# Lightning attention and a leaky-ReLU feed-forward on one core: heads in memory order, and eight more GpSimd dependencies

## The chip, the core and the metric

The kernel runs on one core of a Trainium2 chip. The time is device microseconds of one execution; the figure for a kernel is the median of several runs. A core has a matrix engine (TensorE, PE in the profile, with its weight loads as PEld), VectorE (DVE), ScalarE (ACT), GpSimd (POOL) and SyncE (SP), which here issues the DMA transfers.

## The reference

Linear attention with a decay per head, block by block, then a feed-forward layer on the heads side by side. All results are float32; w_in and w_out come as float64.

```
B, H, S, D = 4, 8, 768, 64            # q, k, v; block = 64
for each block b of a sequence:
    intra = (qb @ kb.T) * Dmask       # Dmask[i, j] = lam ** (i - j) for i >= j
    out   = intra @ vb + (qb * lam ** (i + 1)) @ kv_state
    kv_state = lam ** 64 * kv_state + (kb * lam ** (63 - j)).T @ vb
x = out, heads side by side           # (3072, 512)
h = x @ w_in                          # (512, 2048)
y = max(0.01 * h, h) @ w_out          # (2048, 512)
```

## The kernel before

The 3072 tokens are 24 chunks of 128 (two blocks each, six chunks a sequence, four sequences). Four chunks make a group of 512 tokens.

**Attention of a chunk.** `load_kq` and `load_v` bring k, q and v of a chunk (128 tokens by 8 heads by 64). k and q come in two transfers each: the even heads into the first four places of the tile, the odd heads behind them; v comes in one, in memory order. `transposes` turns k and q on TensorE, two heads side by side on the 128 partitions (in later chunks other transfers and VectorE do it for q, and later for k). `scores` has two TensorE steps: `go` (q times k) and `kv` (k times v, the addition to the state). `outputs` has three: `own` (scores times v), and `inter(0)` and `inter(1)` (state times scaled q), between which an engine reads a corner of the result (`seen_po`). In a steady chunk TensorE runs `own`, `inter(0)`, then `kv` and `go` of the next chunk, then `inter(1)`.

All these steps are made of calls of `quad` (L410), a plain f32 matmul of 64 rows by 64 columns. `rows` (0 or 1) picks the upper or lower 64 partitions of both inputs, `cols` those of the output. A call so uses one of four quarters of the array. The sequence in which the calls are written is the sequence in which TensorE gets them.

`place(h)` says where head h lies in the transposed tiles: which half of the partitions (`a`), which of the four columns (`z`). `own` sends head 2y + hi to the output half hi; `inter(m)` takes those calls for which `t = y % 2 ^ m`.

Around it, GpSimd (VectorE in some early chunks) scales k for the state (`kr`, L591), GpSimd multiplies the state by the decay (L653) and, in later chunks, scales q (L598). VectorE masks the scores (L643), adds to the state (L650) and splits the output into parts for the feed-forward (`xh` on ScalarE, `xl`, `xm`). At the start `factors` (L380) copies `lam` into `lam_h` in the order of the heads, `factors_k` (L383, L386) and `factors_q` (L391, L393) make the tables of decay powers by scans.

**Feed-forward.** Every operand is split into three parts of reduced precision (h, l, m), so each product is three matmuls of 512 columns (`up`, L856; `down`, L922). `to_float32` brings a piece of w_in or w_out as float64 (L787, L790) and turns it into float32 on ScalarE (L799 to L803) and VectorE (L805, L806); `parts` makes the three parts (L813 to L820). The weights' keys in the plan are `w320`, `w321` for the raw pieces and `wh0`, `wl0`, `wm0` and so on for the parts. The result of `up` goes to DRAM and comes back for `down`.

**Order.** All operations are registered by `add(engine, us, fn, reads, writes, ...)` with a planner, `Plan`. `ORDER` lists operations by number and engine, 1296 entries; `emit` takes these first, in this order, and places the rest by planned times. `resolve` turns `reads` and `writes` into dependencies, which the planner uses for its times and for naming buffers. At the end it issues the instructions:

```
for _, _, i, e in self.timeline:
    ...
    fn() if len(ways) == 1 else fn(e)
```

Waits between engines come from the tiles that an instruction itself reads and writes; each engine runs its instructions in the order in which they were issued.

Of the kernel before, what the change touches and what calls it, by code (L numbers as in the profile page):

```python
# [239 lines left out]
def kernel(  # L240
# [27 lines left out]
    FIRST_LOADS = ["k0", "q0", "v0", "k1", "q1", "v1", "w10", "k2", "q2", "v2", "w11", "k3", "q3", "v3"]  # L268
    LOW_PE, MIX_PE = set(), set()
    PAIRS = {"q": set()}  # L270
    QS = 8
    KM = 8
    NRAW = 3
    TURN = 3
    SLACK, GSLACK = 4.0, 2.0
    EARLY_SLACK = 1.0
    GOFIRST = 3
    SUBL, FIRST = 0.75, -8.0

    DV, QD = 10, 8  # L280
    RUNS = {8: (-8.0, 0.8), 10: (-8.0, 0.8), 12: (4.0, 0.0)}
    C4 = P // 4
    HALF = (slice(0, D), slice(D, 2 * D))
    assert NCB % TURN == 0 and D == 64 and KO == HP == 4 and SEQ % C == 0 and NCH % GC == 0 and d_model == T == 512 and NP % 4 == 0

    pool = ctx.enter_context(tc.tile_pool(name="sb", bufs=1))
    psum = ctx.enter_context(tc.tile_pool(name="ps", bufs=1, space=bass.MemoryType.PSUM))
    dram = ctx.enter_context(tc.tile_pool(name="dram", bufs=1, space=bass.MemoryType.DRAM))
    ctx.enter_context(tc.manual_schedule(engines=None))

    def sb(shape, name, dt=F32):
        return pool.tile(shape, dt, name=name, tag=name)
# [27 lines left out]
    def part(n):  # L320
        nonlocal used
        used += n
        assert used <= NA, used
        return att[:, used - n:used]

    ident = part(P)
    kqv_f = [part(2 * H * D + (TURN - 2) * HP * C * (i == 1)) for i in range(3)]
    kqv = [[x[:, i * H * D:(i + 1) * H * D].rearrange("p (h d) -> p h d", h=H) for i in range(2)] for x in kqv_f]
    kTs, qTs, qsTs = ([part(HP * C).rearrange("p (y t) -> p y t", y=HP) for _ in range(2)] for _ in range(3))
    sc = part(2 * HP * C2).rearrange("p (x y t) -> p x y t", x=2, y=HP)  # L330
    state = [part(HP * D).rearrange("p (y d) -> p y d", y=HP) for _ in range(4)]
    decay = part(2 * HP * C2).rearrange("p (x y t) -> p x y t", x=2, y=HP)
    pow_q = part(HP * C2).rearrange("p (y t) -> p y t", y=HP)
    lam_b, lam_h = part(H), part(H)
    lam_p = part(HP)
    zero = part(1)
    seen_po = part(2)
    eye = sc[:, 0, 0, :]


    nc.scalar.dma_start(out=lam_b, in_=lam.partition_broadcast(P))
    make_identity(nc, ident)

    def busy(n, at):

        wide = bank[at].rearrange("p (a t) -> p a t", t=C2)
# [20 lines left out]
    def move(us, fn, reads, writes, issue=0.5, rank=0.0, slack=SLACK, name=None, land=None):  # L367

        if name in FIRST_LOADS:
            rank = FIRST_LOADS.index(name) * 0.01 - 100.0 - plan.rank  # L370
        plan.slack = slack if steady else EARLY_SLACK
        if steady and not rank:
            rank = FIRST
        add("DMA", length(us, issue), fn, reads, writes, rank=rank, land=land or us)
        plan.slack = 0.0


    def factors():
        for i in range(2):
            nc.vector.tensor_copy(lam_h[:, i * HP:(i + 1) * HP], lam_b[:, i::2])  # L380

    def factors_k():
        nc.vector.tensor_tensor(eye, ident[:, 0:C2], ident[:, C2:C], op=ALU.add)  # L383
        for hi in range(2):
            for hp in range(HP):
                nc.vector.tensor_tensor_scan(decay[:, hi, hp, :], _bc(lam_h[:, 2 * hp + hi], 1, C2), eye, 0.0,  # L386
                                             op0=ALU.mult, op1=ALU.add)

    def factors_q():
        for i in range(2):  # L390
            nc.vector.tensor_copy(lam_p[HALF[i]], lam_h[HALF[i], i::2])  # L391
        for hp in range(HP):
            nc.vector.tensor_tensor_scan(pow_q[:, hp, :], _bc(lam_p[:, hp], 1, C2), _bc(zero[:, 0], 1, C2), 1.0,  # L393
                                         op0=ALU.mult, op1=ALU.add)

    pow_k = decay[:, :, :, C2 - 1].rearrange("p hi hp -> p hp hi")
    lam_c = pow_q[:, :, C2 - 1]
    plan.rank = -1.0
    add("DVE", 0.25, factors, [], ["lam"])
    add("DVE", 1.65, factors_k, ["lam"], ["fk", "sc"])  # L400
    add("DVE", 1.2, factors_q, ["lam"], ["fq"])
    if LOW_PE or MIX_PE:
        add("ACT", 0.2, lambda: nc.scalar.activation(out=neg_i, in_=ident, func=AF.Copy, bias=0.0, scale=-1.0), [], [f"wm{LATE_W}", "neg_i"])
    if MIX_PE:
        add("ACT", 0.2, lambda: nc.scalar.activation(out=pos_s, in_=ident, func=AF.Copy, bias=0.0, scale=S), [], [f"wm{LATE_W}", "pos_s"])
    ENG = {"ACT": nc.scalar, "DVE": nc.vector, "POOL": nc.gpsimd}


    def quad(dst, rows, lhsT, rhs, cols, start=False):
        nc.tensor.matmul(dst[HALF[cols]], lhsT=lhsT[HALF[rows]], rhs=rhs[HALF[rows]], start=start, stop=True,  # L410
                         skip_group_check=True)
# [4 lines left out]
    def place(h):  # L416
        i = h // 2 + h % 2 * HP
        return i % 2, i // 2
# [26 lines left out]
    def load_pair(nm, c):  # L445
        b, n, i = of(c)
        y, (dst, keys) = (q if nm == "q" else k)[b, :, n * C:(n + 2) * C, :], pair(nm, c)

        def go():
            for z in range(2):  # L450
                nc.sync.dma_start(out=dst[:, z * HP:(z + 1) * HP].rearrange("p h s d -> p h (s d)"),
                                  in_=y[z::2].rearrange("h (p s) d -> p h (s d)", s=2))
        move(1.75, go, [], keys, issue=1.0, name=f"{nm}{c}")

    def load_kq(c):
        b, n, i = of(c)
        for src, x, nm in ((k, 0, "k"), (q, 1, "q")):
            if paired(nm, c):
                if c % 2 == 0:
                    load_pair(nm, c)  # L460
                continue
            y, (dst, key) = src[b, :, n * C:(n + 1) * C, :], spot(nm, c)

            def go(y=y, dst=dst):
                for z in range(2):
                    nc.sync.dma_start(out=dst[:, z * HP:(z + 1) * HP, :], in_=y[z::2].rearrange("h p d -> p h d"))
            if nm == "k" or c < QD:
                move(1.15, go, [], [key], issue=1.0, name=f"{nm}{c}")
# [33 lines left out]
    def load_subs(c):  # L502
        b, n, i = of(c)
        count = run(c)[1]
        for nm, src, pieces in zip("kq", (k, q), subs(c, count)):
            for sub, lo, hi, keys in pieces:
                add("DVE", 0.0, lambda: None, [], keys)
                for y in range(lo, hi):
                    for a in range(4):
                        h = y // 2 + (2 * y + a // 2) % HP * 2  # L510
                        z = src[b, h, n * C:(n + count) * C, a % 2 * C4:(a % 2 + 1) * C4]
                        o = sub[a * C4:(a + 1) * C4, y - lo, :]
                        move(0.55, lambda o=o, z=z: nc.sync.dma_start(
                                out=o.rearrange("j (m i) -> j m i", i=C4), in_=z.rearrange("(m j) i -> j m i", j=C4)),
                            keys, [f"{nm}s{y}{a}"], issue=SUBL, rank=RUNS.get(c, (4.0, 0.4))[0] + RUNS.get(c, (4.0, 0.4))[1] * (4 * y + a))
# [19 lines left out]
    def transposes(c):  # L535
# [41 lines left out]
        def copies():  # L577
# [3 lines left out]
            if c < DV:  # L581
                ways = (("ACT", "DVE"), (0.6, 0.685)) if c < GC else ("ACT", 0.6)
                add(*ways, lambda e="ACT": copy(e, into, src()), [key], [f"kT{i}"])
                if paired("q", c):
                    add(*ways, lambda e="ACT": copy(e, joined(qTs[i]), apart(zq())), [qkey], [f"qT{i}"])
                elif c < QD:
                    add(*ways, lambda e="ACT": copy(e, qTs[i], zq()), [qkey], [f"qT{i}"])
            kr = tk.rearrange("p (y x) d -> p y x d", x=2)
            nr = slice(0, C2 if n == NCB - 1 else P)
            add(*((("DVE", "POOL"), (0.67, 1.06)) if c < KM else ("POOL", 1.06)),  # L590
                lambda e="POOL": ENG[e].tensor_tensor(kr[nr], kr[nr], _bc(pow_k, 3, D)[nr], op=ALU.mult), ["fk"], [kk], lock=True)  # L591
            m = slice(1 if n == 0 else 0, 2)
            first = c < QS
            eng, e, us, dep = ("DVE", nc.vector, 0.685, [qkey, f"qT{i}"]) if first else ("POOL", nc.gpsimd, 1.28, [f"qT{i}"])

            def scale():
                o, x = (y.rearrange("p y (t i) -> p y t i", t=2)[:, :, m, :] for y in (qsTs[i], zq() if first else qTs[i]))
# [146 lines left out]
    def round_of(c):  # L744
# [18 lines left out]
        if c + 2 < NCH:  # L763
            load_v(c + 2)


    w_in_r = moe_w_in.rearrange("(ko ki) n -> ki ko n", ki=P)
    n_raw = 0

    def to_float32(kind, p, h, dst, key, after=()):  # L770
# [278 lines left out]
```

## Time and profile before

| | |
|---|---|
| median of 3 runs | 607.87 us (606.57, 607.87, 608.01) |
| profiled execution | 605.63 us |
| its span, first to last instruction | 603.8 us |
| TensorE busy | 596.2 us (99%) |
| VectorE, ScalarE, GpSimd busy | 299.1, 209.1, 73.9 us |
| granted TensorE clock | 0.999 |
| DMA engines, mean share in the first 34 us | 0.95 |

A row of a list of groups gives line, engine, operation, written and read tiles, shape, count, then busy time, mean time of one in ns, idle time before and what ended it. The tile `att` holds all of attention's buffers; `po`, `psc`, `pt` and `b` are accumulators. In the chain of waits a row is start, length, engine, tile, line and count; in the timeline it is start, length, then the instruction. A plain f32 matmul shows as two instructions.

### The profile page before, as it was taken

What the parts mean: (1) busy time and instruction counts of PE and PEld (TensorE: products, weight loads), DVE (VectorE), ACT (ScalarE), POOL (GpSimd) and SP (SyncE); (2) the same over time, 40 slices, a digit from 0 to 9 for tenths busy, and PEclk for the clock granted to TensorE, in tenths of its full rate; (3) what the DMA queues carried; (4) which work ended last, traced back from release to release, by engine and by line L of the source; (5) the groups of instructions that cost most, each with busy time, mean ns of one, the idle gap of its engine ahead of it and who ended that gap; (6) DMA issues with size and microseconds to landing.
All of it is one profiled execution on the core that took longest, in us unless ns stands there. A gap on an engine that the chain in (4) does not pass through costs nothing.

```text
span 603.8 us, 12715 instructions
## 1 busy us (share of the span) xinstructions
PE 596.2 (99%) x5362; PEld 491.9 (81%) x5362; DVE 299.1 (50%) x410; ACT 209.1 (35%) x322; POOL 73.9 (12%) x85
## 2 busy tenths in 40 slices
PE   8899999999999999999999999999999999999997
PEld 5788888888888888887888888888888888888886
DVE  6899854450553524344267855353453543534430
ACT  3686752222434433435334421222312313214111
POOL 3332132241322031230000000000000000000000
PEclk9999999999999999999999999999999999999999
DMA  9998887598788798655975834434333333433201
GB/s 215 226 274 214 237 226 201 96 251 202 197 227 215 230 247 233 171 199 194 323 250 194 294 105 132 148 101 139 108 120 125 122 122 123 127 101 128 82 1 69
DMA packets 149993, 105.18 MB, mean 174 GB/s; under 512 B 125872, under 2 KB 126640, under 8 KB 149936
## 3 DMA queue, kind: packets, MB, share of 16 engines
q1 hardware_dynamic: 149648, 104.30, 59.4%
q8 instruction: 42, 0.69, 0.5%
q14 instruction: 15, 0.12, 0.1%
q10 hardware_dynamic: 288, 0.07, 0.0%
HBM read 68.69 MB, written 35.65 MB: 173 GB/s over the span
## 4 chain that ended last, share of the span: by engine, by line
PE 96%; DVE 2%; DMA 0%; issue 0%; ACT 0%; DVEq 0%
PE b L856 33%; PE b L922 16%; PE psc L922 11%; PE po L922 11%; PE pt L856 11%; PE pt L922 5%; PE po L410 4%; PE psc L410 3%; DMA att<-in_lam_dram 0%; PE po L550 0%; PE b L550 0%; DVE att L393 0%; DVE att L386 0%; DVE w L806 0%; DVE att L643 0%
## 5 line engine op out<-in xcount | busy, mean ns | idle before, releaser
L904 DVE SCALAR_TENSOR_TENSOR xl<-att,xh 128x1024 fp32r<-128x1024 f32 x48 | 58.7, 1222 | 125.8 <-ACT xh L903 125.8
L903 ACT ACTIVATE xh<-att 128x1024 fp32r<-128x1024 f32 x48 | 50.9, 1061 | 147.5 <-PE po L922 73.9
L856 PE MATMUL b<-xl,wl 128*128 128x512 f32 (+1 forms) x296 | 78.1, 389 | 0.1
L856 PE MATMUL b<-xm,wm 128*128 128x512 f32 (+1 forms) x296 | 77.9, 390 | 0.0
L856 PE MATMUL b<-xh,wh 128*128 128x512 f32 (+1 forms) x296 | 77.5, 389 | 0.0
L883 ACT ACTIVATE gs<-b 128x512 f32<-128x512 f32 x73 | 42.9, 597 | 95.3 <-PE b L856 85.7
L856 PEld LDWEIGHTS b<-xl,wl 128*128 128x128 f32 x296 | 54.7, 188 | 12.0 <-DVE wl L820 0.9
L856 PEld LDWEIGHTS b<-xh,wh 128*128 128x128 f32 x296 | 54.6, 188 | 11.5 <-DVE att L598 0.3
L856 PEld LDWEIGHTS b<-xm,wm 128*128 128x128 f32 x296 | 54.4, 188 | 11.3
L906 DVE SCALAR_TENSOR_TENSOR xm<-xl,xh 128x1024 fp32r<-128x1024 f32 x48 | 58.8, 1226 | 4.7
L922 PE MATMUL b<-wh,xh 128*128 128x512 f32 x144 | 56.0, 389 | 0.0
L922 PE MATMUL b<-wl,xl 128*128 128x512 f32 x144 | 56.0, 389 | 0.0
L922 PE MATMUL b<-wm,xm 128*128 128x512 f32 x144 | 56.0, 389 | 0.0
L653 POOL TENSOR_TENSOR att<-att 128x256 f32<-128x256 f32 x40 | 29.8, 745 | 112.5 <-DVE att L650 74.0
L922 PE MATMUL psc<-wm,xm 128*128 128x512 f32 (+1 forms) x100 | 38.2, 387 | 0.0
L922 PE MATMUL po<-wm,xm 128*128 128x512 f32 (+1 forms) x100 | 37.9, 384 | 0.0
L922 PE MATMUL psc<-wh,xh 128*128 128x512 f32 x96 | 37.3, 389 | 0.0
L922 PE MATMUL psc<-wl,xl 128*128 128x512 f32 x96 | 37.3, 389 | 0.0
L922 PE MATMUL po<-wh,xh 128*128 128x512 f32 x96 | 37.3, 389 | 0.0
L922 PE MATMUL po<-wl,xl 128*128 128x512 f32 x96 | 37.3, 389 | 0.0
L410 PEld LDWEIGHTS po<-att 64*64 64x64 f32 x1408 | 26.9, 134 | 10.5 <-issue 7.8
L410 PE MATMUL po<-att 64*64 64x64 f32 x1408 | 32.9, 222 | 1.8 <-issue 1.1
(103 smaller groups left out, 859.1 us busy)
## 6 DMA issues: line engine op xcount, KB each, us to landing
att<-g SPq DMA_DIRECT2D x48, 512.0 KB, 3.4
g<-gs SPq DMA_DIRECT2D x47, 512.0 KB, 3.5
raw<-in_moe_w_in_dram SPq DMA_DIRECT2D x16, 512.0 KB, 5.5
raw<-in_moe_w_out_dram SPq DMA_DIRECT2D x16, 512.0 KB, 4.5
out_dram<-gs SPq DMA_DIRECT2D x23, 256.0 KB, 2.1
att<-in_k_dram SPq DMA_DIRECT2D x44, 128.0 KB, 4.0
att<-in_v_dram SPq DMA_DIRECT2D x22, 256.0 KB, 4.2
wo<-w SPq DMA_DIRECT2D x8, 512.0 KB, 3.9
```

Source lines behind the costliest of these rows:

```text
L410: nc.tensor.matmul(dst[HALF[cols]], lhsT=lhsT[HALF[rows]], rhs=rhs[HALF[rows]], start=start, stop=True, skip_group_check=True)
L653: add("POOL", 0.62, lambda new=new, j=j: nc.gpsimd.tensor_tensor(state[(j + 1) % 4], new, _bc(lam_c, 2, D), op=ALU.mult), [f"st{j % 4}", " ...
L856: nc.tensor.matmul(dst, lhsT=w[z][:, kk * 2 * P + f * P:kk * 2 * P + (f + 1) * P], rhs=x[z][:, kk, toks], start=start and kk == 0, stop=kk ...
L883: add("ACT", ns, lambda b=b, r=r: nc.scalar.activation(out=r(), in_=b(), func=AF.Prelu, bias=0.0, scale=1.0, alpha=0.01), [kb], [kg], rank ...
L903: add("ACT", 1.05, lambda: nc.scalar.activation(out=h, in_=graw[j], func=AF.Copy, bias=0.0, scale=NEAR), reads, wr("h"))
L904: add("DVE", 1.215, lambda: nc.vector.scalar_tensor_tensor(l, graw[j], 1.0, h.bitcast(F32), op0=ALU.mult, op1=ALU.subtract), reads + [f"rh ...
L906: add("DVE", 1.215, lambda: nc.vector.scalar_tensor_tensor(m, l.bitcast(F32), -S, h.bitcast(F32), op0=ALU.mult, op1=ALU.add), [f"rh{j}", f ...
L922: nc.tensor.matmul(to[:, cols], lhsT=ring[j][z][:, f * T + tb * P:f * T + (tb + 1) * P], rhs=W[pp][z][:, f * d_model:(f + 1) * d_model][:, ...
```

## The change

k and q of a chunk stay in memory order and come in one transfer each, so `place` and `lam_h` go, and head 2y + a lies in half a, column y of the transposed tiles. `own` sends head h to the output half `column(h)`, and `inter` takes the calls with `t = a ^ m`. The output's heads so lie in other halves for odd y, and the rows of w_in follow: each piece of it is loaded in two transfers of 64 partitions. `BEHIND` names, for three k scalings and five state products on GpSimd, a part of the weights that is added to their `reads`. In `ORDER` five GpSimd entries stand elsewhere among the other engines' (87, 126, 134, 205, 207); taken engine by engine, the order of both lists is the same.

```diff
-    ORDER = [...]
+    ORDER = [...]
...
+    BEHIND = {("k", 2): ["w320"], ("s", 7): ["wm0"], ("k", 5): ["wl0"], ("s", 9): ["wl2"], ("k", 6): ["wl2"], ("s", 12): ["wl3"], ("s", 13): ["wh4"], ("k", 8): ["wl4"]}
...
-    lam_b, lam_h = part(H), part(H)
+    lam_b = part(H)
...
-    def factors():
-        for i in range(2):
-            nc.vector.tensor_copy(lam_h[:, i * HP:(i + 1) * HP], lam_b[:, i::2])
-
...
-                nc.vector.tensor_tensor_scan(decay[:, hi, hp, :], _bc(lam_h[:, 2 * hp + hi], 1, C2), eye, 0.0,
+                nc.vector.tensor_tensor_scan(decay[:, hi, hp, :], _bc(lam_b[:, 2 * hp + hi], 1, C2), eye, 0.0,
...
-            nc.vector.tensor_copy(lam_p[HALF[i]], lam_h[HALF[i], i::2])
+            nc.vector.tensor_copy(lam_p[HALF[i]], lam_b[HALF[i], i::2])
...
-    add("DVE", 0.25, factors, [], ["lam"])
+    add("DVE", 0.0, lambda: None, [], ["lam"])
...
-    def place(h):
-        i = h // 2 + h % 2 * HP
-        return i % 2, i // 2
+    def column(h):
+        return h % 2 ^ h // 2 % 2
...
-                for z in range(2):
-                    nc.sync.dma_start(out=dst[:, z * HP:(z + 1) * HP, :], in_=y[z::2].rearrange("h p d -> p h d"))
+                nc.sync.dma_start(out=dst, in_=y.rearrange("h p d -> p h d"))
...
-                        h = y // 2 + (2 * y + a // 2) % HP * 2
+                        h = 2 * y + a // 2
...
-                lambda e="POOL": ENG[e].tensor_tensor(kr[nr], kr[nr], _bc(pow_k, 3, D)[nr], op=ALU.mult), ["fk"], [kk], lock=True)
+                lambda e="POOL": ENG[e].tensor_tensor(kr[nr], kr[nr], _bc(pow_k, 3, D)[nr], op=ALU.mult), ["fk"] + BEHIND.get(("k", c), []), [kk], lock=True)
...
-                        h = y // 2 + (2 * y + x) % HP * 2
-                        quad(pu[t]()[:, y, :], t, tk[:, 2 * y + x, :], tv[:, h, :], x, start=y == 0)
+                        h = 2 * y + x
+                        quad(pu[t]()[:, y, :], t, tk[:, h, :], tv[:, h, :], x, start=y == 0)
...
-                        [f"st{j % 4}", "fq"], [f"st{(j + 1) % 4}"], lock=True)
+                        [f"st{j % 4}", "fq"] + BEHIND.get(("s", j), []), [f"st{(j + 1) % 4}"], lock=True)
...
         def own():
             for y in range(HP):
-                for hi in range(2):
+                for a in range(2):
                     for t in range(2):
-                        h = 2 * y + hi
-                        a, z = place(h)
-                        quad(po[:, t, y, :], t, tv[:, h, :], sc[:, a, z, :], hi, start=y == 0)
+                        h = 2 * y + a
+                        quad(po[:, t, y, :], t, tv[:, h, :], sc[:, a, y, :], column(h), start=y == 0)
 
         def inter(m):
             for y in range(HP):
-                t = y % 2 ^ m
-                for hi in range(2):
+                for a in range(2):
+                    t = a ^ m
                     if n or t:
-                        a, z = place(2 * y + hi)
-                        quad(po[:, t, y, :], a, state[(2 * c + t - 1) % 4][:, z, :], qsT[:, z, tokens(t)], hi)
+                        quad(po[:, t, y, :], a, state[(2 * c + t - 1) % 4][:, y, :], qsT[:, y, tokens(t)], column(2 * y + a))
...
-    w_in_r = moe_w_in.rearrange("(ko ki) n -> ki ko n", ki=P)
+    w_in_r = moe_w_in.rearrange("(ko ki) n -> ki ko n", ki=C2)
...
-                nc.sync.dma_start(out=r64.rearrange("p (k f) -> p k f", k=2),
-                                  in_=w_in_r[:, 2 * h:2 * h + 2, p * 2 * P:(p + 1) * 2 * P])
+                o = r64.rearrange("p (k f) -> p k f", k=2)
+                for u, rows in enumerate((slice(4 * h, 4 * h + 4, 3), slice(4 * h + 1, 4 * h + 3))):
+                    nc.sync.dma_start(out=o[HALF[u]], in_=w_in_r[:, rows, p * 2 * P:(p + 1) * 2 * P])
```

More of the change, by code (lines that the diff above doesn't have):

```diff
@@ L449, in go @@
         def go():
-            for z in range(2):
-                nc.sync.dma_start(out=dst[:, z * HP:(z + 1) * HP].rearrange("p h s d -> p h (s d)"),
-                                  in_=y[z::2].rearrange("h (p s) d -> p h (s d)", s=2))
+            nc.sync.dma_start(out=dst.rearrange("p h s d -> p h (s d)"), in_=y.rearrange("h (p s) d -> p h (s d)", s=2))
         move(1.75, go, [], keys, issue=1.0, name=f"{nm}{c}")
@@ L464, in go @@
             def go(y=y, dst=dst):
-                for z in range(2):
-                    nc.sync.dma_start(out=dst[:, z * HP:(z + 1) * HP, :], in_=y[z::2].rearrange("h p d -> p h d"))
+                nc.sync.dma_start(out=dst, in_=y.rearrange("h p d -> p h d"))
             if nm == "k" or c < QD:
```

2 lines of the change are left out of this document (1 added, 1 removed).

## The prediction

> **What bounds the kernel now.** I read the page first: who is busy, and the chain that ended last.
>
> ```profile
> span 603.8 us, 12715 instructions
> PE 596.2 (99%) x5362; PEld 491.9 (81%) x5362; DVE 299.1 (50%) x410; ACT 209.1 (35%) x322; POOL 73.9 (12%) x85
> ...
> PE 96%; DVE 2%; DMA 0%; issue 0%; ACT 0%; DVEq 0%
> ```
>
> TensorE is busy for 99% of the span and holds 96% of the chain. A change elsewhere can pay only where TensorE does not yet bind, so the stretches come second:
>
> ```profile
> 0.00:34.00 34.00, 29.98 (x661) 23.31 (x662) 27.23 (x58) 19.06 (x31) 12.43 (x20) 1.00 0.95 231
> 34.00:283.00 249.00, 248.87 (x3314) 205.66 (x3307) 125.88 (x222) 102.81 (x184) 61.45 (x66) 1.00 0.79 211
> ```
>
> The columns are PE, PEld, DVE, ACT and POOL busy, clock, DMA share, GB/s. Only the first 34 us leave TensorE idle (4.0 us). From 34 to 283 us, where 20 of the 24 attention chunks run among the first projection's products, it is full: whatever lengthens its work there is paid at the end. The third view is therefore the chain of one steady chunk, and the groups of the small matmuls of L410:
>
> ```profile
> 102.77 3.63 PE b L856 x16
> ...
> 109.12 0.86 PE po L410 x48
> 109.98 0.93 PE psc L410 x64
> 110.91 0.23 PE po L410 x16
> ```
>
> ```profile
> L410 PE MATMUL po<-att 64*64 64x64 f32 x1408 | 32.9, 222 | 1.8 <-issue 1.1 <-DVE att L682 0.3 <-DVE att L650 0.2
> L410 PE MATMUL psc<-att 64*64 64x64 f32 x1344 | 25.8, 219 | 0.4 <-DVE att L531 0.4
> ```
>
> The code of that chunk has 24 `quad` calls (`own` and half of `inter`), then 32 (`kv` and `go`), then 8. So each call, 64 rows by 64 columns, is two instructions (x64 for 32), and one call takes 0.93 / 32 = 0.029 us. The 64 calls of a chunk add up to 2.02 us.
>
> **How long one `quad` holds its quarter of the array.** The change alters the order in which the quarters are used, so this is the price that matters. I call a quarter rc, r for the half of the input rows and c for the half of the output partitions.
>
> ```profile
> 11.57 1.06 PE b L349 x2
> ```
>
> ```profile
> 11.12 0.45 PE L410 MATMUL po<-att 64*64 64x64 f32 x8
> ...
> 282.18 0.46 PE L410 MATMUL po<-att 64*64 64x64 f32 x16
> ```
>
> The first row (the chain of the start) is two plain f32 matmuls of 512 columns: 0.53 us each, against 0.227 for a 512-column product above (3.63 / 16). For 64 columns that is at most 0.53 / 8 = 0.066 us, so a `quad` of two instructions streams for up to 0.13 us. At 0.029 us a call, four must be streaming at once: all four quarters work, and each takes about 4 x 0.029 = 0.116 us per call. The other two rows (the timeline) confirm it. At 11.12, `inter` of a sequence's first chunk uses one row half alone, quarters 00 01 00 01; from the first start to the last end less one instruction's 0.22 us, four calls take 0.23 us, 0.058 each. At 282.18 both row halves are used and eight calls take 0.24. One row half feeds its two quarters in turn, one call every 0.058 us, and comes back to the same quarter after 0.116.
>
> **The change, part by part.**
>
> *Order of the quarters.* In `own` the old order is 00 10 01 11 for every y. The new `column(h)` swaps the column halves for odd y: 00 10 01 11, then 01 11 00 10, and so on. Seen from one row half, the column sequence was 0 1 0 1 0 1 0 1 and becomes 0 1 1 0 0 1 1 0: three times a call goes to the quarter that its row half has just filled. Such a repeat has to wait until that quarter is free, 0.116 us after the call before instead of 0.058, so it costs 0.058 us. The new `inter` walks 00 11 01 10. Row half 0 starts it on column 0, where `own` ended: a fourth repeat. Row half 1 walks 1 0 1 0, so that `kv` (0 1 0 1) behind the first half and the second half behind `go` each begin with a repeat: five. The two halves may slip by a call:
>
> ```profile
> 139.10 0.27 PE L410 MATMUL psc<-att 64*64 64x64 f32 x1
> 139.14 0.28 PE L410 MATMUL po<-att 64*64 64x64 f32 x3
> ```
>
> Here a `kv` call on the idle row half starts while `inter` still has calls to issue on the other. So I count the worse half, five, and not the six places. The trace has no two neighbours of one row half in one quarter, so the price is bounded: 0 if other calls fill the gap, 0.116 if the whole call is waited for; I take 0.058, which is what the two rates above leave.
>
> [...]
>
> Sum: 12 chunks run their 64 calls in one piece, five repeats each. Eight more (first chunks of a sequence, those before a last chunk, and the last one) have half of an `inter`, half of a `kv` or no next chunk, and I give them four. The four chunks of the first 34 us count half, at four:
>
> ```profile
> by line: PE po L410 12.8%; PE pt L856 8.3%; DMA att<-in_lam_dram 7.9%; PE psc L410 7.7%; issue 5.9%; PE b L856 5.6%; DVE att L393 5.0%; PE b L550 4.8%; DVE att L386 4.6%; DVE w L806 4.3%; DVE att L643 3.8%; DVE att L531 3.8%; PE b L410 3.7%
> ```
>
> This is the chain's share by line in those 34 us, and L410 holds 24% of it, so some of their repeats lie on the path. 12 x 5 + 8 x 4 + 4 x 4 / 2 = 100 repeats x 0.058 = **+5.8 us**. Three per chunk (only `own`) make 24 x 3 x 0.058 = 4.2; six everywhere 8.4.
>
> *Start.* `factors` and its two copies go; the L383 sum behind it needs no `lam` and can run before it lands.
>
> ```profile
> 0.73 2.69 DMA att<-in_lam_dram
> 3.42 0.03 issue
> 3.44 0.24 DVE att L380 x2
> 3.69 0.14 DVE att L383
> 3.82 0.02 issue
> 3.85 1.57 DVE att L386 x8
> ```
>
> The scans of L386 can start at 3.44 instead of 3.85: **-0.4 us** on the chain, whose next pieces are VectorE's too. The bounds are 0 (a transfer of the first chunks is late next, and VectorE waits for it instead) and those 0.4.
>
> *Transfers.* Each k and q of a chunk becomes one transfer, each piece of w_in two, on 64 partitions each.
>
> ```profile
> 0.74 1.01 SPq L466 DMA_DIRECT2D att<-in_k_dram  x2
> ...
> 2.89 0.50 SPq L528 DMA_DIRECT2D att<-in_v_dram  x1
> ...
> 6.76 1.62 SPq L787 DMA_DIRECT2D raw<-in_moe_w_in_dram  x2
> ```
>
> ```profile
> raw<-in_moe_w_in_dram SPq DMA_DIRECT2D x16, 512.0 KB, 5.5
> ...
> att<-in_k_dram SPq DMA_DIRECT2D x44, 128.0 KB, 4.0
> att<-in_v_dram SPq DMA_DIRECT2D x22, 256.0 KB, 4.2
> ```
>
> A v transfer has the size that k's will have and is issued in 0.50 us and landed in 4.2 us, where k needs two issues of 0.5 us and 4.0. Per chunk and tensor SyncE saves 0.5 us; w_in gives back 16 x 0.5. Bytes and packet rows stay the same, and in the first 34 us the DMA engines, not the issues, are the limit (share 0.95). I take 0, between -0.5 and +0.5 us, the time of one issue on the first pieces of w_in; afterwards the full TensorE covers it.
>
> [...]
>
> *GpSimd's waits.* `BEHIND` adds names to the `reads` of eight operations, and `ORDER` moves five GpSimd entries. `Plan.emit` uses `reads` to place operations and to name buffers; then it only calls `fn()`. The instruction touches the same tiles as before, and the order on each engine is the same in both lists, so no instruction gets another wait: 0. If the waits were real, the place to look is here:
>
> ```profile
> 18.16 1.06 POOL L591 TENSOR_TENSOR gs<-gs,att 128x512 f32<-128x512 f32 x1 [1.33 <-PE pt L550]
> 18.30 1.47 DVE L806 CUSTOM_DVE_ANT_0 w<-w,low 128x1024 uint16<-128x1024 uint16 x1
> ...
> 28.16 0.70 DVE L806 CUSTOM_DVE_ANT_0 w<-w,low 128x1024 uint16<-128x1024 uint16 x1
> ```
>
> Behind `w320`, the k scaling of chunk 2 would leave L806 its 0.70 us instead of 1.47 (-0.8 at best), and would delay `kv` of chunk 2 at worst by its own 1.06. Queued behind it on GpSimd are only the state products of L653.
>
> **Sum.** The profiled run took 605.63 us, span and surroundings. 605.6 + 5.8 - 0.4 = 611.0. The median of the runs shown, 607.87, lies 2.24 us above the profiled run; with it the forecast is **613.3 us**.
>
> **The rivals.**
> *Free quarters (no change).* If a call for a free quarter may pass one that waits, the calls per quarter are as many as before and nothing is lost: only the start's 0.4 us remains, 607.5. For it: one row half does pass the other at 139.10. Against it: at 11.12, and in the single-row `kv`, nothing tells that calls pass each other within a row half. [...]
> *Faster.* No repeat costs, and SyncE rather than the DMA engines sets when the first pieces of w_in arrive. They are issued at 6.76, behind k and q of two chunks, so four issues of 0.5 us go ahead of them and TensorE's full stretch starts 2 us sooner: 607.9 - 0.4 - 2.0 = 605.5. It decides if the DMA share of the first 34 us falls well below 0.95 with the same bytes. Against it: that share.
> *Slower still.* A repeat waits for the whole call, 0.116 us: 100 x 0.116 - 0.4 = +11.2, 619.1. Against it: on one row half a call follows in the other quarter after 0.058.
>
> **How the numbers follow.** Forecast 0.64, free quarters 0.20, faster 0.08, slower still 0.08. The forecast's own range is 611 (three repeats) to 616.5 (six, no gain at the start). The range reaches down to the free quarters and a little below for their bounds, 607.0, and up to 616.5; the two outer cases, 0.16, stay out. About 0.3% (1.8 us) is what a measurement of this kernel can tell from no change. Slower takes the forecast, less a little for fewer repeats than counted, and the last rival: 0.71; same 0.20; faster 0.09.
>
> **What would show it.** In the steady chunk the piece of 48 instructions (0.86 us) grows by some 0.2, and the three pieces from 2.02 to about 2.3; the groups of L410 keep their counts and nearly their mean. TensorE stays full from 34 us on, so the 34 to 283 us stretch ends some 5 us later, and the second projection behind it keeps its length. VectorE's scans start at about 3.45. GpSimd's operations show no wait for L806, L818 or L820. The forecast is wrong if the three pieces still add up to 2.02; the start is wrong if the first projection's first product does not move; the reading of `BEHIND` is wrong if a GpSimd operation is seen waiting for one of these lines.

## The result, and the profile after

The changed kernel takes 614.69 us (median of 6 runs, 613.38 to 617.24). The kernel before, run beside it, takes 607.07 us (6 runs, 606.57 to 608.01). The ratio is 1.0130, 95% interval 1.0112 to 1.0148: slower by 7.6 us. The forecast was 613.3 in a range of 607.0 to 616.5, with 0.71 on slower. The number was close by luck: the reason given for it was wrong.

In the changed kernel the lines are a few numbers lower: `quad` is L407, the issues of k and q L459, those of w_in L780, the scans of `factors_k` L383. The page first:

```profile
span 614.0 us, 12674 instructions
PE 599.8 (98%) x5362; PEld 494.2 (80%) x5362; DVE 298.8 (49%) x408; ACT 208.4 (34%) x322; POOL 72.7 (12%) x85
...
PE 87%; DMA 6%; SPq 5%; ACT 1%; issue 1%; POOL 0%; DVE 0%; DVEq 0%; ACTq 0%; POOLq 0%
```

The third line is the chain of waits: TensorE held 96% of it before, with nothing for DMA. Now transfers and SyncE's issues hold 11%. In the profiled execution TensorE is idle for 614.0 - 599.8 = 14.2 us, where it was 7.6. The stretches say where (columns as in the prediction, the last three are granted clock, DMA share and GB/s):

```profile
0.00:34.00 34.00, 27.30 (x563) 20.41 (x563) 22.03 (x48) 14.08 (x23) 10.31 (x18) 0.90 0.98 194
34.00:283.00 249.00, 244.99 (x3299) 202.84 (x3298) 127.77 (x224) 103.50 (x185) 62.36 (x67) 1.00 0.82 208
```

In the first 34 us the DMA engines are as full as before (0.98 against 0.95), but move 194 GB/s in place of 231, and TensorE gets 563 instructions done in place of 661. Of the 6.6 us more of idle time, 2.7 lie in this stretch and 3.9 in the next. The steady chunk, which was to grow, does not. The chain of waits of the changed kernel through one such chunk:

```profile
96.82 0.86 PE po L407 x48
97.68 0.93 PE psc L407 x64
98.61 0.23 PE po L407 x16
```

These are the 0.86, 0.93 and 0.23 us of before, to the hundredth. The time is lost where the transfers are. From the chain of the start:

```profile
11.80 9.57 DMA gs<-in_k_dram
...
30.79 0.88 issue
31.67 0.51 PE b L407 x17
...
33.88 0.60 SPq L780
34.48 0.05 issue
34.53 6.86 DMA raw<-in_moe_w_in_dram
```

The chain runs through a k that takes 9.57 us from its issue to landing, and then through a piece of w_in that takes 6.86. SyncE's issues (L780, L459, L521) hold another 28% of its first 45 us. In the kernel before, once `lam` has landed, VectorE and TensorE hold this part of the chain.

### The profile page after: what moved, and what is told of

The parts are those of the page before. It is cut to its first block, busy times and chain, and to the rows that moved or that the text cites. A ratio compares the mean times of both kernels' runs of the same rounds, so it can differ in the third digit from the quotient of the medians.

```text
span 614.0 us, 12674 instructions
## 1 busy us (share of the span) xinstructions
PE 599.8 (98%) x5362; PEld 494.2 (80%) x5362; DVE 298.8 (49%) x408; ACT 208.4 (34%) x322; POOL 72.7 (12%) x85
## 4 chain that ended last, share of the span: by engine, by line
PE 87%; DMA 6%; SPq 5%; ACT 1%; issue 1%; POOL 0%; DVE 0%; DVEq 0%; ACTq 0%; POOLq 0%
PE b L848 28%; PE b L914 16%; PE psc L914 11%; PE po L914 11%; PE pt L848 9%; PE pt L914 5%; PE po L407 3%; PE psc L407 3%; SPq L506 2%; DMA att<-in_k_dram 2%; DMA raw<-in_moe_w_in_dram 2%; DMA gs<-in_k_dram 2%; SPq L780 1%; SPq L459 1%; SPq L521 1%
## 5 line engine op out<-in xcount | busy, mean ns | idle before, releaser
L875 ACT ACTIVATE gs<-b 128x512 f32<-128x512 f32 x73 | 42.8, 595 | 95.8 <-PE b L848 83.0
L646 POOL TENSOR_TENSOR att<-att 128x256 f32<-128x256 f32 x40 | 28.4, 710 | 117.0 <-DVE att L643 89.7
L407 PEld LDWEIGHTS po<-att 64*64 64x64 f32 x1408 | 26.9, 134 | 11.1 <-issue 8.3
L407 PE MATMUL po<-att 64*64 64x64 f32 x1408 | 32.9, 223 | 2.5 <-issue 1.4
```

The source lines that it names most:

```text
L646: add("POOL", 0.62, lambda new=new, j=j: nc.gpsimd.tensor_tensor(state[(j + 1) % 4], new, _bc(lam_c, 2, D), op=ALU.mult), [f"st{j % 4}", " ...
L875: add("ACT", ns, lambda b=b, r=r: nc.scalar.activation(out=r(), in_=b(), func=AF.Prelu, bias=0.0, scale=1.0, alpha=0.01), [kb], [kg], rank ...
```

## The experiments

Three theories stood at first. **A**: the transfers of w_in to 64 partitions hold the DMA engines longer, and the start is limited by them. **B**: one transfer for a chunk's k or q lands later than two halves. **C**: the order of the quarters, as predicted. All times are medians, with the ratio to the kernel before run beside them, at 606.2 to 606.4 us.

**after_whole_w**: the changed kernel with w_in whole.

```
-    for u, rows in enumerate((slice(4*h, 4*h+4, 3), slice(4*h+1, 4*h+3))):
-        nc.sync.dma_start(out=o[HALF[u]], in_=w_in_r[:, rows, ...])
+    nc.sync.dma_start(out=r64..., in_=w_in_r[:, 2*h:2*h+2, ...])      # 128 partitions
```

> The changed kernel, but each piece of w_in comes in one transfer to 128 partitions again, 16 issues in place of 32. The rows of w_in then lie in their natural order, so the first projection multiplies them with other attention rows; the amount of work is that of the changed kernel. Theory A (the transfers of w_in to 64 partitions hold the DMA engines longer and starve TensorE in the first 60 us): back to 606.5 to 608.5 us, the 2048-byte packets back from 115 to about 98 ns in the mean, and the first 34 us back to about 30 us of TensorE. Theory B (one transfer for k and one for q of a chunk lands later than two halves): stays at 614 to 615. Theory C (the order of the quarters of TensorE, as predicted): stays at 614 to 615.

Measured: 606.77 us, ratio 1.0012 (1.0002 to 1.0023). The 2048-byte packets (4096 of the 7040 are w_in's) fall from 114.5 ns in the mean, in the changed kernel, to 96.1; the kernel before has 98.0.

**before_halves_w**: the kernel before, w_in in halves and nothing else.

```
+    for u in range(2):
+        nc.sync.dma_start(out=o[HALF[u]], in_=w_in_r[HALF[u], 2*h:2*h+2, ...])
```

> The kernel before, with each piece of w_in in two transfers to the two partition halves and nothing else changed. Theory A (transfers to 64 partitions hold the DMA engines): 613 to 615 us, the 2048-byte packets at about 115 ns in the mean. Theory B (one transfer for k and q) and theory C (order of the quarters): both 607.

Measured: 613.79 us, ratio 1.0130 (1.0116 to 1.0144), packets of 114.7 ns. The halves of w_in alone make the whole loss, and without them it is gone: theory A, from both sides.

**before_repeats**: the predicted repeats alone.

```
-    for hi in range(2):
+    for hi in (0, 1) if y % 2 == 0 else (1, 0):
```

> The kernel before, with the two heads of every odd y in own in the other order, so that each row half goes three times per chunk to the quarter it has just filled; nothing else changed. Theory C, by the price of 0.058 us a repeat: 24 x 3 x 0.058 = +4.2, 611 us, and a 64-call piece of 2.0 to 2.1 us from first to last start instead of 1.876. Theories A and B: 607, and the piece stays 1.876.

Measured: 606.05 us, ratio 0.9999 (0.9990 to 1.0007). Its chain of waits through a steady chunk:

```profile
88.06 0.86 PE po L410 x48
88.91 0.93 PE psc L410 x64
89.85 0.23 PE po L410 x16
```

Theory C falls: the 72 repeats of `own` cost nothing that can be seen (0.4 us at the upper end of the interval), against 4.2 us expected. In after_whole_w all the repeats that were predicted are in place, and its ratio is 1.0012. (The piece of "1.876" in the expectation is the same one, taken from the first start to the last start.)

**after_two_kq**: the changed kernel with two transfers each for k and q.

```
-    nc.sync.dma_start(out=dst, in_=y...)
+    for z in range(2):
+        nc.sync.dma_start(out=dst[:, z*HP:(z+1)*HP, :], in_=y[z*HP:(z+1)*HP]...)
```

> The changed kernel, with k and q of a chunk in two transfers of four heads each (heads 0 to 3, heads 4 to 7), still in memory order. Theory B (one long transfer lands later than two halves): 607 to 609 us. Theories A and C: 614 to 615.5.

Measured: 614.55 us, ratio 1.0136 (1.0122 to 1.0151). Theory B does not explain the loss.

**Why a half is slow.** Three theories for that. **N**: two transfers in place of one. **P**: a transfer is slow when all its partitions lie on one side of partition 64, as in both halves. **Q**: one to fewer than 128 partitions is slow, whichever they are. The three are guesses, to be told apart by runs: a transfer to partitions 32 to 95 is a half that lies on both sides.

**before_two_full_w**: two transfers, both to 128 partitions.

```
+    for u in range(2):
+        nc.sync.dma_start(out=o[:, u, :], in_=w_in_r[:, 2*h+u, ...])
```

> The kernel before, with each piece of w_in in two transfers that both go to all 128 partitions (one of the two 128-row blocks each), so 32 issues of 256 KB as in the changed kernel, but none to half of the partitions. Theory N (the number of transfers and issues is the cost): 613 to 615 us, as with the two halves. [...]

Measured: 605.84 us, ratio 0.9991 (0.9981 to 1.0002), packets of 95.0 ns. The same count and size as the halves, and no loss: N falls as it was put; P and Q stand, since both transfers go to all partitions. The lists of DMA issues (line, count, KB each, median us from issue to landing), first with the halves, then with two full ones:

```profile
raw<-in_moe_w_in_dram SPq DMA_DIRECT2D x32, 256.0 KB, 5.1
```

```profile
raw<-in_moe_w_in_dram SPq DMA_DIRECT2D x32, 256.0 KB, 4.0
```

One form of N is left: an issue to 64 partitions holds SyncE longer than one of the same size to 128. Two issues each, from SyncE's timelines, again first with the halves, then with two full ones:

```profile
19.67 1.26 SPq L789 DMA_DIRECT2D raw<-in_moe_w_in_dram  x2
```

```profile
31.83 0.93 SPq L789 DMA_DIRECT2D raw<-in_moe_w_in_dram  x2
```

The time of SyncE on a piece does not go with the loss, though. In the mean of the first eight pieces it is 0.87 us in the kernel before, 1.42 with two full transfers (no loss), 1.68 with the halves (7.6 us lost), 1.89 in before_edge_w below (9.4 us lost) and 2.03 in before_mid_w (7.0 us lost).

**before_mid_w** and **before_edge_w**: three transfers each, of 64, 32 and 32 partitions.

```
mid:   for u in ((32, 96), (0, 32), (96, 128)):
edge:  for u in ((0, 64), (64, 96), (96, 128)):
           nc.sync.dma_start(out=o[slice(*u)], in_=w_in_r[slice(*u), 2*h:2*h+2, ...])
```

> The kernel before, with each piece of w_in in three transfers: partitions 32 to 95, then 0 to 31, then 96 to 127. [...] Theory Q (fewer than 128 partitions is slow, whichever): as before_edge_w, 614 us or more. Theory N (number of transfers): 614 or more as well.

> The kernel before, with each piece of w_in in three transfers again, but partitions 0 to 63, then 64 to 95, then 96 to 127: the same sizes and number as in before_mid_w, and none that spans both sides of partition 64. Theory P: the whole loss, 613 to 615 us, 2048-byte packets at about 115 ns. Theories Q and N: the same time as before_mid_w.

Measured: mid 613.41 us, ratio 1.0109 (1.0090 to 1.0129); edge 615.80, ratio 1.0148 (1.0130 to 1.0165). Packets of 102.8 and 113.6 ns. With the same number and sizes, the version with a range that spans both sides of partition 64 is 2.4 us faster, with intervals that just do not touch, and its packets are shorter by 10.8 ns (those of edge near the 115 expected). This is against Q and N as the whole explanation, and in its direction it agrees with P. In size it does not: were P the whole reason, half of the bytes would lose 3.8 of the 7.6 us, so some 610 us by this estimate, and mid is no faster than the two halves (613.79). Its packets rose by 4.8 ns over the kernel before, where those of the halves rose by 16.7, and most of the loss stayed. Edge, at 613 to 615 expected, came out higher too, 2 us above the halves with intervals that overlap. In mid the other two transfers are still on one side each, and three issues hold SyncE longer than two (2.03 us a piece in mid and 1.89 in edge, against 1.68); how much each adds is open. So P is supported, and not shown in full.

**after_actq_w**: the halves on two queues.

```
-    nc.sync.dma_start(out=o[HALF[u]], ...)
+    (nc.sync, nc.scalar)[u].dma_start(out=o[HALF[u]], ...)
```

> The changed kernel, with the half of w_in that goes to partitions 64 to 127 issued by ScalarE and the other by SyncE, so that both halves are on their way at once. [...] Theory Q: stays at 613 to 615. [...]

Measured: 623.23 us, ratio 1.0273 (1.0259 to 1.0287), packets of 118.0 ns. The 613 to 615 of Q misses. The timeline of ScalarE shows one reason, the waits of TensorE in the first 60 us the next:

```profile
37.53 0.60 ACTq L780 DMA_DIRECT2D raw<-in_moe_w_in_dram  x1
...
44.27 0.80 ACT L793 ACTIVATE low<-raw 128x512 uint16<-128x512 uint32 x1 [4.73 <-DMA raw<-in_moe_w_in_dram]
44.34 0.60 ACTq L780 DMA_DIRECT2D raw<-in_moe_w_in_dram  x1
...
50.10 0.66 ACT L791 ACTIVATE w<-raw 128x512 f32<-128x512 f32 x1 [4.53 <-DMA raw<-in_moe_w_in_dram]
```

```profile
PE b L543 <- ACT gs L875: 7.4, 1, 7.4
```

ScalarE stands still for 4.73 us until a piece lands, issues the next half only then, and stands still again for 4.53 us; TensorE waits 7.4 us for an activation (L875) that ScalarE has queued behind that. So this run cannot tell whether halves on their way together would write faster. The packets, no faster than in the changed kernel (118.0 ns against 114.5), give no sign of it.

**Where it is lost.** Theory **E**: only ahead of about 45 us, where the DMA engines are full (in the kernel before a share of 0.95 up to 34 us and of 0.90 from 34 to 60). Theory **S**: each slow piece costs its share.

```
early:  for u in HALF if p < 4 else (slice(0, P),):       late:  ... if p >= 4 ...
            nc.sync.dma_start(out=o[u], in_=w_in_r[u, 2*h:2*h+2, ...])
```

> The kernel before, with the first 8 of the 16 pieces of w_in (issued from 6.8 to 38.7 us there) in two transfers to the partition halves and the other 8 whole. Theory E (the loss arises only where the DMA engines are full, ahead of about 45 us; later pieces hide behind TensorE): nearly the whole loss of the 16 pieces in halves, 612 to 614 us. Theory S (each slow piece costs its share): about half, 609 to 611 us.

> The kernel before, with the last 8 of the 16 pieces of w_in (issued from 42.5 to 81.1 us there) in two transfers to the partition halves and the first 8 whole. Theory E (only the DMA-bound start loses): 606 to 608 us. Theory S (each slow piece costs its share): 609 to 611 us.

Measured: early 611.94 us, ratio 1.0089 (1.0073 to 1.0104); late 608.00, ratio 1.0023 (1.0013 to 1.0034). 5.7 and 1.8 us, together 7.5 of the 7.6. Most of it comes from the pieces of the start, as E has it; but early lies just below E's range and late at the upper end of its own, so the late pieces are not hidden altogether.

**after_mix_w**: half of the bytes whole.

```
+    nc.sync.dma_start(out=o[:, 0, :], in_=moe_w_in[4*h*C2:(4*h+2)*C2, f])
+    for u in range(2):
+        nc.sync.dma_start(out=o[HALF[u], 1, :], in_=w_in_r[:, 4*h+3-u, f])
```

> The changed kernel, with the half of each piece of w_in whose 128 rows lie next to each other (heads 4h and 4h+1) in one transfer to 128 partitions, and only the other half in two transfers to 64 partitions: three transfers a piece, half of the bytes by halves. [...] If only the issues count: 615 or more; if one slow transfer per piece is enough to delay it: 613 to 615.

Measured: 611.53 us, ratio 1.0076 (1.0055 to 1.0097), packets of 101.3 ns. Half of the bytes, and 60 to 70% of the loss (58% by the two ratios, 70% by the medians); it lies below both ranges. It is the best of the versions that keep the heads in memory order with the rows of w_in that belong to them, and still slower than the kernel before.

**before_one_kq**: the change of k and q alone.

```
-    for z in range(2):
-        nc.sync.dma_start(out=dst[:, z*HP:(z+1)*HP, :], in_=y[z::2]...)
+    nc.sync.dma_start(out=dst, in_=y...)
```

> The kernel before, with k and q of a chunk in one transfer each, heads in memory order, and w_in as before. The heads of k and q then meet other heads of v and other powers of lam; the amount of work is unchanged. As predicted: SyncE saves 0.5 us a transfer and the time stays, 606 to 607.5 us. Theory B in its weak form (two halves of 128 KB land sooner than one of 256 KB at the start, which is the +0.6 us by which after_whole_w lies over the kernel before): 606.5 to 608 us, and lam lands at about 3.9 us instead of 3.4.

Measured: 607.39 us, ratio 1.0016 (1.0006 to 1.0027): 1.2 us slower. The time lies in both ranges, but the interval lies above 1, as the weak form of B has it: SyncE's saved issues buy nothing. It would also account for what is left in after_whole_w (0.6 us).

**The size of the loss** can be estimated from one row of each kernel, the first 60 us. (The DMA share adds up the times of packets and can come out above 1.) First the kernel before, then the changed one:

```profile
0.00:60.00 60.00, 55.84 (x1054) 44.30 (x1056) 52.37 (x94) 37.42 (x63) 19.29 (x26) 1.00 0.93 233
```

```profile
0.00:60.00 60.00, 51.82 (x973) 40.83 (x974) 45.23 (x82) 32.57 (x56) 15.91 (x24) 0.94 0.98 206
```

Then before_halves_w, before_two_full_w, before_mid_w, before_edge_w, before_early_halves_w and after_mix_w:

```profile
0.00:60.00 60.00, 52.34 (x974) 40.97 (x975) 45.37 (x84) 32.56 (x57) 16.27 (x24) 0.94 1.02 205
```

```profile
0.00:60.00 60.00, 56.72 (x1081) 45.13 (x1084) 52.86 (x94) 37.39 (x65) 19.27 (x26) 1.00 0.94 234
```

```profile
0.00:60.00 60.00, 53.13 (x986) 41.54 (x987) 47.76 (x87) 33.78 (x58) 16.56 (x24) 1.00 0.92 212
```

```profile
0.00:60.00 60.00, 50.85 (x977) 39.45 (x978) 45.79 (x84) 33.14 (x58) 16.69 (x24) 1.00 1.00 207
```

```profile
0.00:60.00 60.00, 51.51 (x978) 40.65 (x979) 45.81 (x84) 33.79 (x58) 16.67 (x24) 0.97 1.05 216
```

```profile
0.00:60.00 60.00, 52.96 (x983) 41.77 (x984) 47.17 (x84) 34.45 (x60) 16.62 (x24) 0.97 0.94 213
```

By 60 us the changed kernel has moved (233 - 206) x 60 us = 1.62 MB less than the kernel before. At its own 206 GB/s it needs 7.9 us more to bring them; 7.6 us were measured. The same working for the others (the last six from the same view, their rows not shown):

| kernel | GB/s to 60 us | late by, us | measured, us |
|---|---|---|---|
| before_two_full_w | 234 | -0.3 | -0.6 |
| after_mix_w | 213 | 5.6 | 5.3 |
| before_early_halves_w | 216 | 4.7 | 5.7 |
| before_mid_w | 212 | 5.9 | 7.0 |
| before_halves_w | 205 | 8.2 | 7.6 |
| before_edge_w | 207 | 7.5 | 9.4 |
| before_repeats | 233 | 0 | -0.1 |
| before_late_halves_w | 232 | 0.3 | 1.8 |
| before_one_kq | 232 | 0.3 | 1.2 |
| after_whole_w | 229 | 1.0 | 0.6 |
| after_two_kq | 209 | 6.9 | 8.4 |
| after_actq_w | 175 | 19.9 | 16.8 |

It comes out within 2 us, except where ScalarE's waits hold the transfers back (after_actq_w). So in these kernels what is missing by the end of the crowded stretch shows at the end nearly in full. The rate by itself does not tell why the bytes are missing; the runs above do.

## Why the prediction was right and wrong, step by step

**Order of the quarters, +5.8 us: wrong, it is 0.** The failed step is the price of 0.058 us for a repeat. The lower end of its bound, 0, is what holds. The pieces to compare stay at 0.86, 0.93 and 0.23 us, in the changed kernel and with the repeats alone. The *Free quarters* rival was right that nothing is lost; its way to that, calls that pass each other, is not shown, since a quarter may also be free sooner than I worked out. Nor does any run show a price for the six places that the upper end of the range counts: with all of them in place after_whole_w has a ratio of 1.0012.

The groups of L407 keep their counts and nearly their means, as said (222 and 219 ns before), which was no test of the repeats:

```profile
L407 PE MATMUL po<-att 64*64 64x64 f32 x1408 | 32.9, 223 | 2.5 <-issue 1.4 <-ACT att L673 0.6 <-DVE att L673 0.3
...
L407 PE MATMUL psc<-att 64*64 64x64 f32 x1344 | 26.2, 222 | 2.1 <-DMA att<-in_v_dram 1.1 <-POOL att L584 1.0
```

**Transfers, 0 between -0.5 and +0.5: wrong, it is the whole loss of 7.6.** The failed step is that the pieces of w_in were priced by their issues, with "bytes and packet rows stay the same". The bytes stay, but the time that an engine takes for each does not (114.5 ns in the mean for a 2048-byte packet against 98.0), and the same paragraph quoted the row that makes this count: a DMA share of 0.95 in the first 34 us. The +0.5 end took one issue as the whole price of a half; no run shows that, and the halves alone cost 7.6 (before_halves_w). Where no row priced the operation, the bound above should have been transfers that land clearly later on a queue that is already full (5.1 us in before_halves_w in place of 4.0 in before_two_full_w for the same 256 KB, as it turned out), not one issue.

In k and q the saving on SyncE was right (the first k holds it 0.44 us, the two halves held it 1.01) and without use. From issue to landing, one 256 KB transfer of k takes 4.8 us in the median where one of 128 KB took 4.0, and those into `gs` at the start 8.6 where they took 5.7; the list of DMA issues after:

```profile
raw<-in_moe_w_in_dram SPq DMA_DIRECT2D x32, 256.0 KB, 5.5
...
att<-in_k_dram SPq DMA_DIRECT2D x22, 256.0 KB, 4.8
...
gs<-in_k_dram SPq DMA_DIRECT2D x2, 256.0 KB, 8.6
...
att<-in_lam_dram ACTq DMA_DIRECT2D x1, 4.0 KB, 3.1
```

**Start, -0.4: wrong.** The last row says why. `lam` takes 3.1 us in place of 2.7, and the scans start when it lands. That longer transfers beside it hold it up is likely, since it takes 3.0 to 3.1 us in before_one_kq, after_whole_w and after_mix_w, and 2.7 to 2.9 in the kernels with two; but only the delay is shown. VectorE's timeline of the changed kernel, then of after_two_kq:

```profile
3.89 1.57 DVE L383 TENSOR_TENSOR_SCAN att<-att 128x64 f32<-128x64 f32 x8 [2.33 <-DMA att<-in_lam_dram]
```

```profile
3.53 1.56 DVE L383 TENSOR_TENSOR_SCAN att<-att 128x64 f32<-128x64 f32 x8 [1.97 <-DMA att<-in_lam_dram]
```

They were to start at 3.45 and start at 3.89, against 3.85 before. With two transfers for k and q the gain of `factors` is there, at 3.53, but the whole time (614.55 against 614.69) does not show it: the bound of 0 ("a transfer is late next") is what holds. These are single executions; in before_repeats, where `factors` is as before, the scans start at 4.05.

**GpSimd's waits, 0: right.** In the trace GpSimd's 85 instructions come in the same order as before, by operation and tiles, and after_whole_w, with the same `BEHIND` and `ORDER`, has a ratio of 1.0012. The longest waits of GpSimd after are those of before, on the same kinds of work, and no weight part is among them:

```profile
POOL att L646 <- DVE att L643: 89.7, 26, 9.2
POOL att L584 <- DMA att<-in_k_dram: 32.1, 8, 8.8
POOL att L591 <- DVE att L515: 24.2, 3, 16.7
```

**TensorE full from 34 us on: wrong.** The 34 to 283 us stretch has 4.0 us of idle in place of 0.1: what did not arrive at the start is short behind it.

**The sum** came near the result by luck: a cost that does not exist (5.8) stood in place of one that was left out (7.6). Over the median that it started from it adds 5.4 us, where 7.6 were measured. Two ends of its own range are added up loosely: with three repeats a chunk its terms give 611.7, not 611, and with six and no gain at the start 616.3, not 616.5.

## What to carry over

A transfer that was cut by partitions was not the same transfer twice (7.6 us here), while one cut along the free dimension cost nothing (ratio 0.9991): in this kernel, keep all 128 partitions in each where the DMA engines are full (a share of 0.95 in the first 34 us). There, price a change of a transfer by the engine time of its packets (114.7 ns against 98.0 here), not by its issue, and look for the bytes moved by the end of that stretch: what is missing then, over the rate, is an estimate of the loss. A forecast that comes out right is no evidence for its mechanism; the row that was to grow (here the steady chunk) has to be looked at by itself.

## What was not expected of the hardware

Two transfers of 256 KB to all partitions landed in 4.0 us each in the median, two to the partition halves in 5.1, with the rest of the kernel the same, and the packets of other transfers slowed with them: the 256-byte ones from 18.6 ns in the mean in the kernel before to 20.4 in before_halves_w, over the whole run. An issue to 64 partitions held SyncE 0.61 us in the median (before_halves_w), one of the same size to 128 partitions 0.43 (before_two_full_w). Plain f32 matmuls of 64 by 64 went twice in turn to the same quarter of TensorE at no cost that could be seen (ratio 0.9999).

In the profiled execution of the changed kernel the granted clock fell for a while. From 15 to 25 us:

```profile
15.00:20.00 5.00, 2.25 (x48) 1.64 (x52) 2.12 (x6) 2.81 (x6) 1.26 (x2) 1.00 0.90 180
20.00:25.00 5.00, 3.96 (x59) 3.33 (x56) 3.92 (x6) 2.82 (x5) 0.42 (x1) 0.51 0.88 193
```

After 2.75 us of idle in five, the next five ran at 0.51. No rule follows: in before_edge_w TensorE was idle for 6.78 us of the first 34, against 6.70 in the changed kernel, and the clock of that stretch was 1.00, against 0.90. Nor is it needed for the loss: the profiled runs of after_two_kq and before_edge_w had a clock of 1.00 throughout the start, and spans of 612.6 and 613.5 us.
